# Bias rows of twelve groups instead of eleven ahead of attention, shifted code, and the products of the smallest experts regrouped

## The chip, the cores and the metric

One core of a Trainium2 chip runs the whole program in one launch. The engines that matter here are TensorE (PE in the rows, its weight loads PEld), VectorE (DVE), ScalarE (ACT), GpSimd (POOL) and SyncE (SP), which issues most of the DMAs. The metric is the device time of one execution in microseconds; lower is better.

## The reference

Three layers, one after the other, all in float32:

```python
# 1. attention, B=2, H=8, S=576, D=64, with a learned bias of the relative position
scores = (q @ k.T) / sqrt(D)
x = log1p(|i - j|) / log1p(max(i, 1))              # per row i and column j
bias = relu(x * w1 + b1) @ w2                      # 32 hidden values -> 8 heads
attn = exp(s - max(s)); attn /= attn.sum() + 1e-9  # s = scores + bias
x = attn @ v                                       # -> 1152 tokens x 512

# 2. gated dense layer, 512 -> 1536 -> 512
x = (silu(x @ w_gate) * (x @ w_val)) @ w_out

# 3. top-1 routing over 8 experts, capacity 288 rows, 512 -> 1024 -> 512
e = argmax(x @ gate); out[row] = softmax(x @ gate)[e] * relu(x @ w1[e]) @ w2[e]
```

## The kernel before, in words

**Bias rows.** The bias depends on i only through a factor of the row, so the kernel works on 36 groups of 16 rows. `span(R)` (L103) gives the columns of group R: 400 for R=11, 384 for R=12, 368 for R=13, 352 for R=14. A group takes four VectorE instructions (`bias_t4`, L116, "B" in the tables below), a TensorE product (`bias_mm`, L134, "M", and "MR" for columns past 512), two ScalarE instructions that write the 128x591 tile `bo` (`bias_evac`, L153 and L160, "BE" and "BR"), and a DMA of that tile to the DRAM buffer `bias_d` (L164). Tiles `bo` rotate over four buffers (L145), so a group's L153 writes into the buffer of the group four earlier in the order and needs that group's DMA to have read it. `load_bias` (L168) brings 128 query rows of two heads from `bias_d` back as `bias_sb`, in three DMAs (L175 to L177). Groups are taken in the order R = 16 to 23, 8 to 15, 24 to 31, 0 to 7, 32 to 35; the first eight complete the first 128 query rows.

**Attention.** A lead loop (L377) does the first LEAD = 11 groups (R = 16 to 23 and 8 to 10), interleaved with the first score product, then `keep_warm` (L352, 12 small products with an unused result) and the four B of the next group. A loop of 36 units (L417) follows. Unit u is one pair of heads for 128 query rows: score product "Q" (`qk`, L196, for unit u+1), score plus bias with a row minimum on VectorE ("S0", "S1", L213), exponential on ScalarE ("E0", "E1", L221), row sum and reciprocal ("A" L227, "R" L230), normalising on GpSimd ("N0", "N1", L234), transposes on TensorE ("Ta", "T", "Tb", L263 and L274, of unit u-1) with copies out ("V0", "V1", "Va", "Vb", L280, L285, L287), and the product with v ("AV", L299, of unit u-2, 20 rows of the trace each). Unit u also makes the product and the evacuation of the bias group LEAD+u and the four B of group LEAD+u+1, as long as there are groups; after that come units without any, whose VectorE and ScalarE slots hold the first steps of the next layer's weight decoding (`job`, "JD", "JA", from unit JOB0 on). All instructions stand in the order in which tables of names list them (`FIRST[0]` and `FIRST[1]` for units 0 and 1, `ORDER` for the rest, `LATE0` and `LATE` for units without bias work); each engine runs its own instructions in that order.

**Code position.** `addr_align` (L357) and a table `ALIGN` (L530, used by `align(n)`, L1081) pad the instruction stream of an engine at a few places: a modulus, an offset from the start of a block, and limits.

**Experts.** Experts are sorted by their number of rows. On the inputs here two large ones come first, then one of middle size, one with q=2, and two with q=4, the smallest; the last two are empty. For q=4 `few1` (L1128) does the first product `ps_sh` (L1139), the transposes of the next expert's rows (`transpose_x`, `ps_x`, L1072) and `slots` (L1009), which has a product `ps_c` (L1013), its copy to `sx` on ScalarE (L1014) and a chain on GpSimd that computes the output rows (L1019 to L1024); then VectorE applies relu to `ps_sh` (`hst`, L1150), TensorE transposes it (`ps_st`, L1154) and VectorE copies it to `sht` (L1158). `few2` (L1167) does the second product `ps_sy` (L1179), and `finish` scales it on VectorE (`ob`, L1034) and scatters it to the output (L671).

Of the kernel before, what the change touches and what calls it, by code (L numbers as in the profile page):

```python
# [26 lines left out]
    "R:1 V0:2 S0 AV:3 S1 B E0 V1:2 N0 MR Vb:2 B N1 BR XH:3 E1 B M Ta XL:3 Va Q B T Tb A BE"  # L27
).split()
FIRST = [
    "B B B S0 S1 B E0 MR M BR E1 Q A BE".split(),  # L30
    "R:1 S0 S1 B E0 N0 MR B N1 BR E1 B M Q B Ta Va T Tb A BE".split(),
]
LATE0 = "R:1 V0:2 S0 S1 AV:3 V1:2 JD JD E0 N1 N0 Vb:2 E1 A R XH:3 JA Q XL:3 T".split()
LATE = (
# [5 lines left out]
    "N0 N1 V0:2 V1:2 AV:3 K0 K0 XH:3 XL:3 T T9:2 V2:2 ACT V0 V1 K0 K0 K0 K1 G0 K1 AV T9 XH V2 XL K1 K1 K1 K0 K0 K1 K1 G1".split(),  # L40
    "AV XH XL".split(),
]
LEAD = 11
IDLE = (38, 12)
RAW0 = 18
ZERO0 = 8
JOB0 = 25
GEO0 = 400


def attention(tc, ident, shape, qd, kd, vd, wb, geo, xh, xl, late):
    nc = tc.nc
    B, H, S, D = shape
    P = 128
# [14 lines left out]
    with ExitStack() as ctx:  # L69
# [284 lines left out]
        spare, raw0 = [], []  # L354
        ran = {("Q", 0)}
        with tc.manual_schedule():
            nc.tensor.addr_align(256, offset=164, max_nops=0)  # L357
            keep_warm(IDLE[0], I16)
            first = wk.tile([P, S], F32, tag="bt", name="first", bufs=12)
            nc.scalar.activation(first[:, :1], ident[:, :1], AF.Identity)  # L360
# [15 lines left out]

            for n in range(LEAD):  # L377
                R = groups[n]
# [38 lines left out]
            for u in range(NU + 2):  # L417
# [18 lines left out]
                R, ahead = (groups[n] if n < NG else None for n in (LEAD + u, LEAD + u + 1))  # L436
# [71 lines left out]
def moe_kernel(ctx, tc, shape, qd, kd, vd, wb, geo, wg, wv, wo, g2, e1, e2, ebase, desc, tri, out, cap):  # L508
    nc = tc.nc
    P = 128  # L510
    B, H, S, D = shape
# [15 lines left out]
    BATCHES = (2, 4, 6, 7)  # L527
    FIX, QUADS = 2, 4
    EARLY = 5
    ALIGN = {"tensor": (256, 7, 131, 0, 0), "vector": (128, 45, 100, 0, 0), "scalar": (128, 65, 100, 0, 0)}  # L530
    TINY = float(np.array([0x38100000], np.uint32).view(np.float32)[0])

    cst = ctx.enter_context(tc.tile_pool(name="cst", bufs=1))
# [506 lines left out]
    xd0 = {}  # L1040
# [28 lines left out]
    def transpose_x(e):  # L1069
        if e < NE:  # L1070
            for kc in range(KC):
                nc.tensor.transpose(px[e][:, kc * P:(kc + 1) * P], xd0[e][:, kc * P:(kc + 1) * P], ident)  # L1072
            nc.scalar.copy(xt[e].rearrange("p k t -> p (k t)"), px[e])
# [54 lines left out]
    def few1(e, q):  # L1128
        w = weights(e)
        x = xt[e]  # L1130
        n, fw = P // q, F2 // q
        nk = fw // P
        ph = []
        for s in range(fw // 256):
            ps = eps.tile([P, 512], F32, tag="h", name="ps_sh")
            for kc in range(KC):
                for g in range(q):
                    f = g * fw + s * 256
                    i = nc.tensor.matmul(  # L1139
                        ps[g * n:(g + 1) * n, :256], x[:, kc, :n], w[f // 256][:, kc, :],  # L1140
                        start=kc == 0, stop=kc == KC - 1, skip_group_check=True,
                    )
                    own(i, e, f // 256)
            ph.append(ps)
        to = next_rows(e, q) if q == 4 else None
        h = hst[:, 0]
        pt = []
        for s in range(fw // 256):
            c = slice(s * 256, (s + 1) * 256)
            nc.vector.tensor_scalar_max(h[:, c], ph[s][:, :256], 0.0)  # L1150
            ps = eps.tile([P, 512], F32, tag="t", name="ps_st")
            for k in range(2):
                o = (2 * s + k) * P
                nc.tensor.transpose(ps[:, k * P:(k + 1) * P], h[:, o:o + P], ident)  # L1154
            pt.append(ps)
        ht_ = hid[e][2]
        for s in range(fw // 256):
            nc.vector.tensor_copy(  # L1158
                ht_[:, 2 * s:2 * s + 2].rearrange("p k g t -> p (k g t)"), pt[s][:, :2 * P]
            )  # L1160
        return to

    def next_rows(e, q):
        transpose_x(e + 1)
        return slots(xd0[e], e, 0, q)

    def few2(e, q, to):  # L1167
        w = weights(e)
        n, fw = P // q, F2 // q
        nk = fw // P  # L1170
        to = to or next_rows(e, q)
        ht_ = hid[e][2].rearrange("p k g t -> p (k g t)")[:, :nk * P].rearrange("p (k g t) -> p k g t", k=nk, g=q)
        ps = eps.tile([P, 512], F32, tag="y", name="ps_sy", bufs=3)
        seq = [(k, g) for k in range(nk) for g in range(q)]
        dw = DM // q
        for i, (k, g) in enumerate(seq):
            f = g * nk + k
            for d in range(q):
                m = nc.tensor.matmul(  # L1179
                    ps[d * n:(d + 1) * n, :dw], ht_[:, k, g, :], w[4 + f // 2][:, f % 2, d * dw:(d + 1) * dw],  # L1180
                    start=i == 0, stop=i == len(seq) - 1, skip_group_check=True,
                )
                own(m, e, 4 + f // 2)
        finish(ps, to, dw)
# [122 lines left out]
    with tc.manual_schedule():  # L1307
# [51 lines left out]
        with ExitStack() as nest:  # L1359
            for e in range(FIX, NE):  # L1360
                nest.enter_context(tc.If(ns[e] > (M1 // 2 if e >= QUADS else 0), label=f"q{e}"))
                with tc.If(ns[e] <= M1, label=f"d{e}"):
                    if e < NE - 1:
                        hint(f"q{e + 1}")
                    few2(e, 2, few1(e, 2))
                    load_next(e, False)
            align(4)
        with ExitStack() as nest:  # L1368
            for e in range(QUADS, NE):
                nest.enter_context(tc.If(ns[e] > 0, label=f"z{e}"))  # L1370
                with tc.If(ns[e] <= M1 // 2, label=f"s{e}"):  # L1371
                    few2(e, 4, few1(e, 4))
                    load_next(e, False)


# [80 lines left out]
```

## Time and profile before

| | |
|---|---|
| three runs | 517.97, 519.69, 520.3 us, median 519.69 |
| the profiled execution | 517.11 us, its span 515.5 us, granted clock 0.999 |
| PE busy | 496.0 us (96%) |
| DVE busy | 371.4 us (72%) |
| ACT busy | 266.5 us (52%) |
| POOL busy | 102.3 us (20%) |

The span is the time from the first to the last recorded instruction of the profiled execution; the device time is 1.6 us more. Times of rows below count from the start of the span. Attention ends at about 165 us, the dense layer follows, and the experts take the last part.

### The profile page before, as it was taken

What the parts mean: (1) busy time and instruction counts of PE and PEld (TensorE: products, weight loads), DVE (VectorE), ACT (ScalarE), POOL (GpSimd) and SP (SyncE); (2) the same over time, 40 slices, a digit from 0 to 9 for tenths busy, and PEclk for the clock granted to TensorE, in tenths of its full rate; (3) what the DMA queues carried; (4) which work ended last, traced back from release to release, by engine and by line L of the source; (5) the groups of instructions that cost most, each with busy time, mean ns of one, the idle gap of its engine ahead of it and who ended that gap; (6) DMA issues with size and microseconds to landing.
All of it is one profiled execution on the core that took longest, in us unless ns stands there. A gap on an engine that the chain in (4) does not pass through costs nothing. (4 is left out here: it accounts for less than half of the span.)

```text
span 515.5 us, 12030 instructions
## 1 busy us (share of the span) xinstructions
PE 496.0 (96%) x4414; PEld 413.4 (80%) x4414; DVE 371.4 (72%) x931; ACT 266.5 (52%) x607; POOL 102.3 (20%) x218
## 2 busy tenths in 40 slices
PE   7989999999999999999999999999999899999885
PEld 3467777677868999979999889999777788897654
DVE  6789999997997999996799827644346654644521
ACT  5599899998876445454543203522322344635410
POOL 1054444444552100000000000000013230512112
PEclk9999999999999999999999999999999999999999
DMA  7797779989612944353231000000015799954740
GB/s 267 264 347 276 242 252 330 318 291 343 151 47 59 314 160 133 122 186 100 83 123 41 2 0 1 1 1 0 1 43 167 287 361 405 382 192 130 279 182 10
DMA packets 49937, 88.82 MB, mean 172 GB/s; under 512 B 7954, under 2 KB 27412, under 8 KB 49856
## 3 DMA queue, kind: packets, MB, share of 16 engines
q1 hardware_dynamic: 48416, 84.78, 48.6%
q0 software_dynamic: 1296, 3.03, 1.5%
q8 instruction: 40, 0.66, 0.5%
q14 instruction: 41, 0.34, 0.2%
q10 hardware_dynamic: 144, 0.02, 0.0%
HBM read 66.73 MB, written 22.15 MB: 172 GB/s over the span
## 5 line engine op out<-in xcount | busy, mean ns | idle before, releaser
L587 PE MATMUL ps_gv<-xh,hl 128*128 128x384 f32 x528 | 134.9, 336 | 0.0
L587 PEld LDWEIGHTS ps_gv<-xh,hl 128*128 128x128 f32 x528 | 95.4, 188 | 0.1
L587 PE MATMUL ps_gv<-xl,hl 128*128 128x384 f32 x264 | 88.7, 336 | 0.0
L880 PE MATMUL ps_o<-hl,hh 128*128 128x512 f32 x216 | 72.9, 404 | 0.0
L116 DVE TENSOR_SCALAR bt<-geo_sb 128x320 f32<-128x320 f32 (+17 forms) x144 | 58.4, 454 | 0.0
L221 ACT ACTIVATE e_sb<-e_sb,mn 128x576 f32<-128x576 f32 x72 | 56.4, 784 | 3.9 <-DVE mn L213 3.6
L234 POOL TENSOR_SCALAR e_sb<-e_sb,rs 128x576 f32<-128x576 f32 x72 | 53.3, 751 | 17.5 <-DVE rs L230 14.3
L213 DVE CUSTOM_DVE_ANT_0 e_sb<-ps_s,bias_sb 128x576 f32<-128x576 f32 x72 | 51.6, 751 | 4.3 <-DMA bias_sb<-bias_d 2.3
L671 POOL DMA_INDIRECT disp<-y,rsi x9 | 9.0, 999 | 223.9 <-DVE rs L828 207.8
L587 PEld LDWEIGHTS ps_gv<-xl,hl 128*128 128x128 f32 x264 | 49.6, 188 | 0.1
L880 PEld LDWEIGHTS ps_o<-hl,hh 128*128 128x128 f32 x216 | 40.6, 188 | 10.1 <-issue 1.4
L299 PE MATMUL ps_x<-et,vn 128*64 128x128 f32 (+1 forms) x800 | 47.5, 267 | 0.7 <-DVE xl L317 0.7
L196 PE MATMUL ps_s<-kst,qst 64*128 64x288 f32 (+1 forms) x320 | 46.2, 423 | 0.5 <-DVE mn L213 0.5
L597 ACT CAST hh<-sg 128x384 fp32r<-128x384 f32 x36 | 18.4, 512 | 47.8 <-DVE sg L596 47.7
L299 PEld LDWEIGHTS ps_x<-et,vn 128*64 128x64 f32 x800 | 39.3, 137 | 3.8 <-DVE xl L317 1.0
L880 PE MATMUL ps_o<-hl,hlo 128*128 128x512 f32 x105 | 42.0, 400 | 0.0
L570 ACT CAST hl<-dg 128x512 fp32r<-128x512 f32 x32 | 19.1, 620 | 39.9 <-PE ps_o L880 21.6
L196 PEld LDWEIGHTS ps_s<-kst,qst 64*128 64x128 f32 (+1 forms) x320 | 27.5, 178 | 6.3 <-DVE mn L213 2.2
L263 PEld LDWEIGHTS ps_t<-ident,e_sb 64*128 64x128 f32 x576 | 25.5, 139 | 4.8 <-issue 0.9
L596 DVE TENSOR_TENSOR sg<-ps_gv,sg 128x384 f32<-128x384 f32 x35 | 19.3, 552 | 12.6 <-PE ps_gv L587 12.6
L595 DVE TENSOR_TENSOR sg<-ps_gv,sg 128x384 f32<-128x384 f32 x35 | 19.3, 552 | 10.7 <-ACT sg L594 10.4
L565 ACT ACTIVATE dg<-raw 128x512 f32<-128x512 f32 x32 | 21.0, 673 | 10.0 <-DVE hl L571 7.0
(231 smaller groups left out, 931.4 us busy)
## 6 DMA issues: line engine op xcount, KB each, us to landing
eraw<-e SPq DMA_DIRECT2D x24, 512.0 KB
bias_d<-bo SPq DMA_DIRECT2D x36, 295.5 KB
raw<-e SPq DMA_DIRECT2D x16, 512.0 KB
raw<-wo SPq DMA_DIRECT2D x12, 512.0 KB
raw<-wg SPq DMA_DIRECT2D x11, 512.0 KB
raw<-wv SPq DMA_DIRECT2D x11, 512.0 KB
disp<-zero SPq DMA_DIRECT2D x9, 520.0 KB
bias_sb<-bias_d SPq DMA_DIRECT2D x16, 288.0 KB
```

The source lines that it names most:

```text
L116: nc.vector.tensor_scalar(t[:, :m], dist_sb[:, :m], nbp[:, r:r + 1], None, ALU.max)
L196: nc.tensor.matmul(pss[j][i, half, :HS], qst[c * B + bb][d, p, i], kst[d, bb * NP + p, half * HS:(half + 1) * HS], start=True, stop=True, ...
L213: nc.vector.tensor_tensor_reduce(out=e[:, j, :].rearrange("p (a n) -> p a n", a=2), in0=ps[:, :, :HS], in1=bias_sb[c, p][:, j, :].rearrang ...
L221: nc.scalar.activation(e[:, j, :], e[:, j, :], AF.Exp, bias=mn[:, j:j + 1], scale=-1.0, accum_out=sm[:, j:j + 1])
L234: nc.gpsimd.tensor_scalar(e[:, j, :], e[:, j, :], rs, 1.0, ALU.mult, ALU.mult)
L263: nc.tensor.transpose(tp_t[u, h][:, n * HP:(n + 1) * HP], e[r, n * P:(n + 1) * P], ident[r, r])
L299: nc.tensor.matmul(ps[j * D:(j + 1) * D, o:o + n], vn[:, p, bb, jc, j * D:(j + 1) * D], et[:, t0:t0 + n], start=jc == NF, stop=jc == NF - ...
L565: lambda: nc.scalar.activation(g, hi32.bitcast(F32), AF.Square),
L587: nc.tensor.matmul(ps[:, :TN], w_[:, n, kc, :], x_[:, kc, t * TN:(t + 1) * TN], start=i == 0, stop=i == 3 * KC - 1,)
L595: nc.vector.tensor_tensor(sg, pss[0][:, :TN], sg, ALU.mult)
L596: nc.vector.tensor_tensor(sg, pss[1][:, :TN], sg, ALU.mult)
L880: nc.tensor.matmul(ps, ht_cols(f, a, tg), wot[f][b_], start=i == 0, stop=i == len(ops) - 1)
```

## The change

Five things are changed. LEAD becomes 12, so group R=11 moves from unit 0 into the lead loop, each later group moves to the unit before, and unit 24 becomes one without bias work; JOB0 goes from 25 to 24 with it. The tables of units 0 and 1 are written in another order: unit 0 has its four B later (S0 first), and BE after E1; unit 1 begins with S0 and only then R of unit 0. `keep_warm` after the lead loop has 4 products instead of 12. The code offset of TensorE before attention goes from 164 to 100, and VectorE's offset at `align(2)` from 100 to 109. In the two q=4 experts the copy of 128x256 to `sht` becomes two of 128x128, and `slots` moves from behind the transposes `ps_x` to behind the transposes `ps_st`; for the q=2 expert the order is as before.

```diff
 FIRST = [
-    "B B B S0 S1 B E0 MR M BR E1 Q A BE".split(),
-    "R:1 S0 S1 B E0 N0 MR B N1 BR E1 B M Q B Ta Va T Tb A BE".split(),
+    "MR M S0 S1 E0 B BR B E1 BE Q B B A".split(),
+    "S0 R:1 S1 B E0 N0 MR B N1 BR E1 B M Q B Ta Va T Tb A BE".split(),
 ]
-LEAD = 11
-IDLE = (38, 12)
+LEAD = 12
+IDLE = (38, 4)
-JOB0 = 25
+JOB0 = 24
...
-            nc.tensor.addr_align(256, offset=164, max_nops=0)
+            nc.tensor.addr_align(256, offset=100, max_nops=0)
...
-    ALIGN = {"tensor": (256, 7, 131, 0, 0), "vector": (128, 45, 100, 0, 0), "scalar": (128, 65, 100, 0, 0)}
+    ALIGN = {"tensor": (256, 7, 131, 0, 0), "vector": (128, 45, 109, 0, 0), "scalar": (128, 65, 100, 0, 0)}
...
-        to = next_rows(e, q) if q == 4 else None
+        if q == 4:
+            transpose_x(e + 1)
         h = hst[:, 0]
...
-            nc.vector.tensor_copy(
-                ht_[:, 2 * s:2 * s + 2].rearrange("p k g t -> p (k g t)"), pt[s][:, :2 * P]
-            )
-        return to
-
-    def next_rows(e, q):
-        transpose_x(e + 1)
-        return slots(xd0[e], e, 0, q)
-
-    def few2(e, q, to):
+            if q == 2:
+                nc.vector.tensor_copy(
+                    ht_[:, 2 * s:2 * s + 2].rearrange("p k g t -> p (k g t)"), pt[s][:, :2 * P]
+                )
+            else:
+                for k in range(2):
+                    nc.vector.tensor_copy(
+                        ht_[:, 2 * s + k].rearrange("p g t -> p (g t)"), pt[s][:, k * P:(k + 1) * P]
+                    )
+
+    def few2(e, q):
...
-        to = to or next_rows(e, q)
+        if q == 2:
+            transpose_x(e + 1)
+        to = slots(xd0[e], e, 0, q)
```

TensorE's order at the head, in the lead loop and unit 0 (`ps_w` is the product of a group of the lead loop, `ps_b` that of a group in the unit loop, `ps_s` a score product; - before, + now):

```order
 L196 MATMUL ps_s<-kst,qst 128x288 x4
 L134 MATMUL ps_w_371<-bt,wb_sb 32x416 x4
-L352 MATMUL ps_idle<-ident 128x128 x12
-L134 MATMUL ps_b<-bt,wb_sb 32x400 x4
-L196 MATMUL ps_s<-kst,qst 128x288 x4
+L134 MATMUL ps_w_388<-bt,wb_sb 32x400 x4
+L352 MATMUL ps_idle<-ident 128x128 x4
 L134 MATMUL ps_b<-bt,wb_sb 32x384 x4
 L196 MATMUL ps_s<-kst,qst 128x288 x4
```

The product of the group with 400 columns now stands in the lead loop, ahead of the small products, and unit 0 has that of 384 columns.

ScalarE's order at the same place (`bo` is the bias tile, the rows on `e_sb` are the exponentials of units 0 and 1):

```order
 L160 ACTIVATE bo<-ps_w_371,ncst,geo_sb 128x175
-L221 ACTIVATE e_sb,sm<-e_sb,mn 128x576 x2
-L153 ACTIVATE bo<-ps_b,ncst,geo_sb 128x400
-L160 ACTIVATE bo<-ps_b,ncst,geo_sb 128x191
-L221 ACTIVATE e_sb,sm<-e_sb,mn 128x576 x2
-L280 COPY et<-ps_x 128x64
+L153 ACTIVATE bo<-ps_w_388,ncst,geo_sb 128x400
+L160 ACTIVATE bo<-ps_w_388,ncst,geo_sb 128x191
+L221 ACTIVATE e_sb,sm<-e_sb,mn 128x576 x2
 L153 ACTIVATE bo<-ps_b,ncst,geo_sb 128x384
```

The evacuation of the group with 400 columns moved ahead of the two exponentials of unit 0, and behind these now stands that of the group with 384 columns.

TensorE's order in the first of the q=4 experts, with what each row waits for; before:

```order
L1072 MATMUL ps_x<-ident,xd_5476 128x128 x3
L1013 MATMUL ps_c<-xd_5475,copies_3131 128x2 [waits DMAHW3_49,Activation_49]
L1154 MATMUL ps_st<-ident,hst 128x128 [waits DVE_49]
L1154 MATMUL ps_st<-ident,hst 128x128
L1179 MATMUL ps_sy<-eraw_5515,sht 32x128 [waits DMAHW2_49,DVE_49]
```

and now:

```order
L1072 MATMUL ps_x<-ident,xd_5466 128x128 x3
L1155 MATMUL ps_st<-ident,hst 128x128 [waits DVE_49]
L1155 MATMUL ps_st<-ident,hst 128x128
L1013 MATMUL ps_c<-xd_5465,copies_3121 128x2 [waits DMAHW3_49,Activation_49]
L1183 MATMUL ps_sy<-eraw_5505,sht 32x128 [waits DMAHW2_49,DVE_49]
L1183 MATMUL ps_sy<-eraw_5505,sht 32x128 x3
```

The product `ps_c` went from ahead of the two transposes of `hst` to behind them.

## Rows read from the trace of the kernel before

**Rows 1.** Busy time by stretch: stretch, length, engines' busy us (instructions), PEclk, DMA share, GB/s.

```profile
20.00:30.00 10.00, 8.80 (x81) 5.70 (x73) 6.22 (x20) 5.64 (x14) 2.11 (x4) 1.00 0.96 297
320.00:360.00 40.00, 40.00 (x233) 40.00 (x232) 19.46 (x35) 12.75 (x25) 0.00 (x0) 1.00 0.00 1
...
514.00:515.50 1.50, 0.00 (x0) 0.00 (x0) 0.00 (x0) 0.00 (x0) 0.00 (x0) 0.80 0.00 0
```

**Rows 2.** Timeline of TensorE: start, length, line, operation, xcount [idle before <- releaser].

```profile
34.32 1.31 PE L299 MATMUL ps_x<-et,vn 128*64 128x128 f32 x20
...
57.28 1.31 PE L299 MATMUL ps_x<-et,vn 128*64 128x128 f32 x20
...
131.24 1.31 PE L299 MATMUL ps_x<-et,vn 128*64 128x128 f32 x20
...
147.41 1.31 PE L299 MATMUL ps_x<-et,vn 128*64 128x128 f32 x20
```

**Rows 3.** Timeline of VectorE, S0 of units 0 and 24.

```profile
23.38 0.76 DVE L213 CUSTOM_DVE_ANT_0 e_sb<-ps_s,bias_sb 128x576 f32<-128x576 f32 x1 [1.99 <-DMA bias_sb<-bias_d]
...
117.30 0.76 DVE L213 CUSTOM_DVE_ANT_0 e_sb<-ps_s,bias_sb 128x576 f32<-128x576 f32 x1 [0.30 <-DMA bias_sb<-bias_d]
```

**Rows 4.** Timeline of SyncE, issues of the bias DMAs near 22 and 106 us.

```profile
19.01 0.32 SPq L175 DMA_DIRECT2D bias_sb<-bias_d  x1
...
22.59 1.40 SPq L164 DMA_DIRECT2D bias_d<-bo  x3
...
28.32 0.91 SPq L176 DMA_DIRECT2D bias_sb<-bias_d  x1
...
106.65 0.77 SPq L164 DMA_DIRECT2D bias_d<-bo  x1
114.34 0.33 SPq L175 DMA_DIRECT2D bias_sb<-bias_d  x1
```

**Rows 5.** Timeline of ScalarE, evacuation of the bias group of unit 0.

```profile
26.38 0.67 ACT L153 ACTIVATE bo<-ps_b,ncst,geo_sb 128x400 f32<-128x400 f32 x1
26.95 0.50 ACT L160 ACTIVATE bo<-ps_b,ncst,geo_sb 128x191 f32<-128x191 f32 x1
```

**Rows 6.** Timeline of TensorE, bias products of units 1 and 2.

```profile
27.50 0.85 PE L134 MATMUL ps_b<-bt,wb_sb 128*32 128x384 f32 x8 [0.64 <-ACT bo L160]
...
31.04 0.82 PE L134 MATMUL ps_b<-bt,wb_sb 128*32 128x368 f32 x8 [0.72 <-ACT bo L160]
```

**Rows 7.** Busy time by stretch again, columns as in the first group.

```profile
23.40:26.60 3.20, 2.64 (x17) 1.13 (x16) 1.84 (x5) 1.86 (x5) 0.00 (x0) 1.00 1.02 363
```

**Rows 8.** DMA issues: line, count, KB each.

```profile
bias_d<-bo SPq DMA_DIRECT2D x36, 295.5 KB
...
bias_sb<-bias_d SPq DMA_DIRECT2D x16, 288.0 KB
```

**Rows 9.** DMA queues from 19.5 to 20.5 us: packets, MB, share of 16 engines' time.

```profile
q8 instruction: 1, 0.02, 6.0%
```

**Rows 10.** Timeline of TensorE in the two q=4 experts.

```profile
500.96 0.38 PE L1013 MATMUL ps_c<-xd,copies 32*128 32x2 f32 x2
501.27 0.44 PE L1154 MATMUL ps_st<-ident,hst 128*128 128x128 f32 x2
502.23 1.95 PE L1179 MATMUL ps_sy<-eraw,sht 128*32 128x128 f32 x64 [0.52 <-DVE sht L1158]
...
507.33 0.44 PE L1154 MATMUL ps_st<-ident,hst 128*128 128x128 f32 x2
```

**Rows 11.** Timeline of VectorE in the second of these experts.

```profile
506.85 0.42 DVE L1150 TENSOR_SCALAR hst<-ps_sh 128x256 f32<-128x256 f32 x1 [2.19 <-PE ps_sh L1139]
...
510.37 0.35 DVE L1034 TENSOR_SCALAR ob<-ps_sy,sx 128x128 f32<-128x128 f32 x1 [2.14 <-PE ps_sy L1179]
```

**Rows 12.** Groups by line and shape, VectorE: count | busy us, mean ns | idle before.

```profile
L285 DVE COPY et<-ps_t 128x512 f32<-128x512 f32 x36 | 24.4, 677 | 0.4 <-PE ps_t L263 0.4
L1158 DVE COPY sht<-ps_st 128x256 f32<-128x256 f32 x4 | 1.7, 424 | 1.5 <-PE ps_st L1154 1.5
```

More of the change, by code (lines that the diff above doesn't have):

```diff
@@ L1364, in moe_kernel @@
                         hint(f"q{e + 1}")
-                    few2(e, 2, few1(e, 2))
+                    few1(e, 2)
+                    few2(e, 2)
                     load_next(e, False)
@@ L1371, in moe_kernel @@
                 with tc.If(ns[e] <= M1 // 2, label=f"s{e}"):
-                    few2(e, 4, few1(e, 4))
+                    few1(e, 4)
+                    few2(e, 4)
                     load_next(e, False)
```

## The prediction

> **What bounds the kernel now.** I read the busy time by stretch first. In a stretch of the dense layer TensorE is busy for all of its 40 us at a granted clock of 1.00; at the head, from 20 to 30 us, it has 8.80 of 10 while the DMA share is 0.96 [rows 1]. So TensorE sets the time except at the two ends: at the head it is held by DMAs, and at the tail by short chains through VectorE and ScalarE. The clock falls only in the last 1.5 us, with no TensorE work left [rows 1]. That narrows the change to four places: the head, the bias units of attention, one late DMA wait, and the two smallest experts.
>
> Next comes TensorE's timeline of the product with v, which occurs once a unit and so gives the period. From 34.32 to 57.28 six units take 22.96 us, 3.83 each, and these hold a bias product; from 131.24 to 147.41 five units without one take 16.17 us, 3.23 each [rows 2]. VectorE's timeline then shows two waits for bias tiles: 1.99 us before the first S0 and 0.30 us before that of unit 24 [rows 3]. SyncE's timeline tells which DMA is meant, and the last views read are the experts' timelines.
>
> **The change part by part.** The sum is made against the profiled execution's 517.11 us and then carried to the median 519.69, which is 2.58 us higher; the rows explain no part of that gap.
>
> *One bias unit fewer.* The product, the evacuation and the four B of one group leave the unit loop. The groups that follow move one unit up, so one unit of 3.83 us becomes one of 3.23: -0.60 [rows 2]. The work that left stands in the lead loop: the product takes the place of idle products on TensorE, and ScalarE and VectorE wait there, VectorE for 1.99 us [rows 3]. It costs nothing as long as the first S0 still waits for its DMA. If a unit is held by VectorE and not by TensorE, the gain may come out at nothing.
>
> *The wait at unit 24.* Its bias tile was loaded at 114.34, when the write of the last group it needs, issued at 106.65, had landed [rows 4]. That write is now issued one unit, about 3.8 us, earlier. The 0.30 us go [rows 3]: -0.30, at worst 0, if another engine is late at the same point.
>
> *The first evacuation in unit 0.* Here the change adds a wait. Before, unit 0 evacuated the 400-column group from 26.38 on [rows 5], into a `bo` buffer read out long before. Now it evacuates the 384-column group, whose buffer is that of the fourth group before it, and that group's DMA is the first of the three issued from 22.59 on [rows 4], behind two loads of 128 query rows. When does it land? S0 of unit 0 starts at 23.38 [rows 3] with half of the first load there; left are the other half of 288 KB, the second load of 576 KB and the write of 295.5 KB [rows 8], 1160 KB. From 23.40 to 26.60 the DMAs moved 363 GB/s [rows 7], so 3.2 us carry 1160 KB, and the write lands at 26.6 if the queues run evenly: +0.2 against 26.38. From the other side: the L176 load at 28.32 [rows 4] waits, in SyncE's order, for the same write, so by 28.3 it was there: at most +1.9. Behind the evacuation ScalarE holds the exponentials of unit 1, and TensorE's next bias product waits for it, by 0.64 us at 27.50 and again by 0.72 at 31.04 for the one after [rows 6]; score product, transposes and the next evacuation follow in that chain, so its delay reaches the end undiminished. I take 27.0, +0.6, nearer to the even landing than to the bound, since the DMA share stays at about 1 [rows 7].
>
> The Trainium skill ("DMA: Bandwidth & Descriptors", section "Why a DMA increments its semaphore by 16 and not by 1") says that a copy is spread over up to 16 engines which finish independently, and that only the full count means that all data has landed. By that rule the slowest engine decides and the even estimate of 26.6 is too early; with the rule the term is +0.6 or more, without it +0.2. The trace of before shows only the bounds.
>
> *Rest of the head.* S0 of unit 0 no longer has three B before it in its unit, but all four of its group stand in the lead loop: one more ahead of a wait of 1.99 us [rows 3], so 0. R after S0 in unit 1: 0, since S0 of unit 0 is what unit 0's exponentials wait for and R of that unit is not due before. Four idle products instead of twelve: 0, they ran in TensorE's idle time.
>
> *Code offsets.* From 19.5 to 20.5 us the trace has one instruction fetch, and it took 6.0% of 16 engines [rows 9], 0.96 us of one DMA engine. It falls into the first bias load, issued at 19.01 [rows 4]. With the offset of 100 the boundary moves to a later instruction, out of this load: if the load's slowest engine was the one with the fetch, S0 of unit 0 starts up to 0.8 us sooner; if the fetch then lies on the write that the evacuation waits for, up to 0.96 later. No row tells which. I take 0, with -0.8 and +1.0 as ends. VectorE's offset moves by nine instructions: 0, within the same ends.
>
> The Trainium skill ("Runtime: NRT & Kernel Launch", section "Instruction fetch mechanics") has an engine fetch blocks of 256 instructions with a DMA queue of its own while it executes. By it the offset is worth nothing; the row shows a fetch that takes a whole microsecond of one DMA engine while the others carry data, by which it is worth up to 0.96.
>
> *The two smallest experts.* In the first, `ps_c` runs from 500.96 and holds up the transposes, which start at 501.27: without it they start 0.31 earlier; `ps_c` then runs in the time in which TensorE waits for the copy, 0.52 us [rows 10]. In the second the transposes, at 507.33, wait for `hst`, which ends at 507.27 [rows 10, 11], so nothing there. The copy: 128x512 takes 677 ns and 128x256 424 [rows 12], 0.99 ns a column; a half of 128 columns takes 424 - 127 = 297 ns. The second half lies beside the first half of the products, 32 of 64 rows or 0.97 us [rows 10]. So -0.13 in each expert, and -0.31 - 0.26 = -0.57 in all. On GpSimd the chain for the output rows starts about half a microsecond later; it has until the result is scaled, at 510.37 in the second expert [rows 11], 2 us after the products begin. Bounds: a half copy at half the price, -0.31 - 0.42 = -0.73; a half that costs as much as the whole, -0.31.
>
> Sum: -0.60 - 0.30 + 0.60 + 0 - 0.57 = -0.87, so 516.24 for the profiled execution, and 519.69 - 0.87 = **518.8 us** on the median.
>
> **The rivals.**
>
> *The evacuation holds unit 0 (slower).* Place: L153 of unit 0. If the write lands only at 28.3, the term is +1.9 instead of +0.6, and the sum +0.43: 520.1 us. It decides from a start of 27.9 on (26.38 and the 1.47 that the other terms save). For it: the DMA share of about 1 [rows 7] and the load that waits until 28.32 [rows 4]. Against it: that SyncE row is an upper bound, since it may have waited for its place in the issue order alone.
>
> *The fetch leaves the first load (faster).* S0 of unit 0 starts 0.8 sooner, and the write lands with the queues at 26.6 or before, so the term of the evacuation is +0.2 or less: -0.60 - 0.30 + 0.2 - 0.57 - 0.8 = -2.07, 517.6 us. For it: the 6.0% [rows 9] inside a load that VectorE waits for. Against it: nothing shows that this engine was the last.
>
> *The clock falls in the head.* TensorE has eight products fewer in its idle time. If it were granted the lower level, 1.2 instead of 2.4 GHz, for the bias products of units 1 and 2, these would take 0.85 + 0.82 us more [rows 6]: -0.87 + 1.67 = +0.80, 520.5 us. For it: 0.80 granted in the idle last 1.5 us; against it: 1.00 from 20 to 30 us, in spite of 1.2 us idle [rows 1].
>
> The Trainium skill ("TensorE: Matmul & The Clock Gate", section "HAM oscillation — how this bites in real kernels") says that waits for data between products can bring the clock down. The trace agrees only at its end; at the head none is seen.
>
> *The unit gains nothing.* If VectorE bounds the units that now move, only the other terms stay: -0.27, 519.4 us.
>
> **How the numbers follow.** Chances: the forecast 0.50, with a range of its own from 518.0 to 519.6; the evacuation 0.14; the fetch 0.20; the clock 0.04; no gain from the unit 0.12. A difference under 0.5% (2.6 us) can't be told from no change with this kernel. To be faster by more, under 517.1, the fetch's gain must meet the other terms at their ends, or the true level of before be below its median: 0.16. To be slower by more, over 522.3, takes the fetch on the late write and the clock together: 0.05. The range reaches from 516.8, the fetch with the tail's best end and the write early, to 520.9, the evacuation with part of a fetch on its write.
>
> **What the profile after would show.** Right: 23 units with 3.8 and a first unit of 3.2 one earlier, S0 of unit 24 without a wait; L153 of unit 0 at about 27.0 with a DMA of `bias_d` as its releaser; in both experts the wait before `ps_sy` at some 0.4 and `ps_c` inside it. Wrong: L153 after 27.9, a fetch that moves S0 of unit 0 off 23.4, a granted clock under 1.00 before 40 us, or a new wait on GpSimd before the scatter.

## The result: slower, at the head by the clock as much as by the wait

The changed kernel has a median of 521.78 us over 14 runs (519.51 to 524.86), the kernel before 518.02 over 14; the ratio is 1.0066, 95% interval 1.0043 to 1.0089. Measured again (run 9 below) it is 1.0053 [1.0027, 1.0079]. Forecast were 518.8 us and a range up to 520.9: the time lies outside and on the other side. The forecast stood on the median of three runs, 519.69; over 14 runs the kernel before is 1.67 us below that, so the medians differ by +3.76 us where -0.87 was forecast.

The profiled execution of the changed kernel took 519.51 us, its span 517.9, 2.4 us over the profiled one before. So it is one of the two quickest of the 14; what the others have on top comes up with run 9. Three places of it answer to the prediction. ScalarE at the head (start, length, line, operation, in brackets the idle time before it and what ended that):

```profile
24.14 0.78 ACT L221 ACTIVATE e_sb<-e_sb,mn 128x576 f32<-128x576 f32 x1
...
27.81 0.67 ACT L153 ACTIVATE bo<-ps_b,ncst,geo_sb 128x384 f32<-128x384 f32 x1 [2.80 <-DMA bias_d<-bo]
```

Unit 0's evacuation stands idle for 2.80 us, and the DMA that ends this is the write of the tile of group R=8, from the buffer that it reuses. (R=8 is the ninth group in the order; the expectations below count from zero and call it the eighth.) Before, its counterpart began at 26.38 with no wait [rows 5]. TensorE at the same place:

```profile
23.34 2.06 PE L196 MATMUL ps_s<-kst,qst 64*128 64x288 f32 x8
28.95 1.20 PE L134 MATMUL ps_b<-bt,wb_sb 128*32 128x368 f32 x8 [3.56 <-ACT bo L160]
30.08 2.29 PE L196 MATMUL ps_s<-kst,qst 64*128 64x288 f32 x8
...
37.05 1.31 PE L299 MATMUL ps_x<-et,vn 128*64 128x128 f32 x20
```

It has nothing to do for 3.56 us, where it had 0.64 [rows 6]; then the product of 368 columns takes 1.20 us instead of 0.82, and the score product behind it 2.29, where a later one (at 35.32) takes 1.24. The windows tell why (stretch, length, busy us of PE, PEld, DVE, ACT and POOL with instruction counts, granted clock, DMA share, GB/s):

```profile
26.00:27.00 1.00, 0.00 (x0) 0.00 (x0) 1.00 (x6) 0.00 (x0) 0.76 (x2) 1.00 1.04 399
27.00:28.00 1.00, 0.00 (x0) 0.00 (x0) 1.00 (x3) 0.19 (x1) 0.79 (x1) 1.00 1.20 369
28.00:29.00 1.00, 0.05 (x4) 0.05 (x8) 0.61 (x2) 1.00 (x3) 0.00 (x0) 1.00 0.92 333
29.00:30.00 1.00, 1.00 (x8) 0.10 (x8) 0.00 (x0) 1.00 (x3) 0.00 (x0) 0.63 1.08 359
30.00:31.00 1.00, 1.00 (x8) 0.79 (x6) 0.17 (x1) 0.41 (x2) 0.22 (x1) 0.50 0.91 344
31.00:32.00 1.00, 1.00 (x6) 0.63 (x6) 0.00 (x0) 0.00 (x0) 0.99 (x2) 0.50 1.06 395
32.00:33.00 1.00, 1.00 (x20) 0.81 (x16) 0.60 (x1) 0.49 (x2) 0.48 (x1) 0.66 1.01 356
```

TensorE idles through 26 to 28, and just as it starts again the granted clock falls to 0.50, which is 1.2 GHz, for some three microseconds. From 20 to 30 us the kernel before had 1.00 [rows 1]. The first product with v starts at 37.05 instead of 34.32 [rows 2]: +2.73 us at the head. Of these 1.43 are the later start of the evacuation (27.81 against 26.38), and 1.30 come between it and that product (9.24 us against 7.94).

From there the units win part of it back. The dense layer's first product after attention, before and now:

```profile
166.72 0.44 PE L587 MATMUL ps_gv<-xh,th 128*128 128x384 f32 x1
168.66 0.44 PE L587 MATMUL ps_gv<-xh,th 128*128 128x384 f32 x1
```

That is +1.94, so the unit loop gave 0.79. The small drift up to the middle expert is +0.22. Then comes a place of which the prediction said nothing would happen, TensorE's wait at the branch into the q=2 expert (TensorE's waits near the end: line, releaser, total, times, longest):

```profile
PE ps_sh L1139 <- DVEq L1366: 2.4, 1, 2.4
PE ps_mh L1203 <- DVEq L1349: 1.2, 1, 1.2
PE ps_sh L1139 <- DVEq L1363: 1.1, 1, 1.1
```

The first of these was 1.64 us in the kernel before (timeline of TensorE there):

```profile
488.05 3.67 PE L1139 MATMUL ps_sh<-raw,xt 128*64 128x256 f32 x32 [1.64 <-ACTq L1362]
```

Now VectorE's sequencer is the last to come, and the wait is 2.37 us: +0.73. The two smallest experts do what was forecast:

```profile
503.91 0.44 PE L1155 MATMUL ps_st<-ident,hst 128*128 128x128 f32 x2
504.28 0.38 PE L1013 MATMUL ps_c<-xd,copies 32*128 32x2 f32 x2
504.73 1.95 PE L1183 MATMUL ps_sy<-eraw,sht 128*32 128x128 f32 x64
...
510.23 0.38 PE L1013 MATMUL ps_c<-xd,copies 32*128 32x2 f32 x2
510.68 1.95 PE L1183 MATMUL ps_sy<-eraw,sht 128*32 128x128 f32 x64
```

`ps_c` lies inside the wait for the copy, and `ps_sy` shows no idle time where it had 0.52 [rows 10]; the shift against before goes from +2.89 at the first of these experts to +2.39 at the last product. Sum: 2.73 - 0.79 + 0.22 + 0.73 - 0.50 = 2.39, the difference of the spans (2.4).

### The profile page after: what moved, and what is told of

Read it like the earlier page. It is cut to its first block, busy times and chain, and to the rows that moved or that the text cites. A ratio compares the mean times of both kernels' runs of the same rounds, so it can differ in the third digit from the quotient of the medians.

```text
span 517.9 us, 11999 instructions
## 1 busy us (share of the span) xinstructions
PE 494.6 (96%) x4397; PEld 411.4 (79%) x4397; DVE 371.1 (72%) x933; ACT 266.5 (51%) x606; POOL 102.3 (20%) x218
## 5 line engine op out<-in xcount | busy, mean ns | idle before, releaser
L196 PEld LDWEIGHTS ps_s<-kst,qst 64*128 64x128 f32 (+1 forms) x320 | 27.4, 182 | 6.6 <-DVE mn L213 1.3
L134 PE MATMUL ps_b<-bt,wb_sb 128*32 128x512 f32 (+11 forms) x192 | 23.9, 569 | 4.3 <-ACT bo L160 4.2
## 6 DMA issues: line engine op xcount, KB each, us to landing
bias_d<-bo SPq DMA_DIRECT2D x36, 295.5 KB, 4.1
```

Of the source, the lines that this page charges most:

```text
L134: nc.tensor.matmul(ps[t4 * GW:(t4 + 1) * GW, :m1 - m0], wb2, bt_t[R, t4][:, m0:m1], start=True, stop=True)
L196: nc.tensor.matmul(pss[j][i, half, :HS], qst[c * B + bb][d, p, i], kst[d, bb * NP + p, half * HS:(half + 1) * HS], start=True, stop=True, ...
```

## The experiments

Theory A: the head loses by the wait for the write of R=8, and once more because TensorE idles behind it and its clock falls. Rival B: the clock falls for want of the eight idle products. Rival C: the code offsets carry the loss. Ratios are those to the kernel before on the same chip, with 95% intervals. They need not equal the quotient of two medians (up to 0.3% apart). Runs 1 to 4, 5 to 8, 9 to 12 and 13 to 16 shared a chip each. Five kernels were measured twice: four repeat their ratio within 0.13%, but that of runs 12 and 14 differs by 0.54%. So a single difference of half a per cent between two chips shows little; pairs on one chip count for more.

**Run 1, the evacuation into a buffer nobody has used.**

```diff
-                bo_t[R] = wk.tile([P, WIDE], F32, tag="bo", name="bo", bufs=4)
+                bo_t[R] = (
+                    wk.tile([P, NB_ * P], F32, tag="et", name="bo", bufs=3)[:, :WIDE] if R == groups[LEAD]
+                    else wk.tile([P, WIDE], F32, tag="bo", name="bo", bufs=4)
+                )
```

> The changed kernel, but the 384-column group of unit 0 is evacuated into a buffer of another tag (et) that nobody has used yet, so its first activation waits for no DMA. Theory A (the loss is that wait, and TensorE's clock falls because TensorE idles behind it): the evacuation starts right after the second exponential of unit 0, at 25.0 instead of 27.8; TensorE's longest idle before 32 us falls from 3.56 to about 1.5 us; granted clock 1.00 until 40 us; the first product with v starts near 34 instead of 37.05; about 517 us, some 1 below the kernel before and 4 to 5 below the changed one. Rival B (the clock falls for the eight idle products that are gone): clock still at 0.5 to 0.7 near 30 us, 520 us or more. Rival C (the loss is in the code offsets): as the changed kernel, 521.8 us.

Measured: 518.50 us, 0.9993 [0.9970, 1.0015], 1.5 us over what theory A forecast. The head is as theory A has it: no wait, evacuation at 25.49, first product with v at 33.28 instead of 37.05, granted clock 1.00 from 26 to 50 us.

```profile
26.61 0.83 PE L134 MATMUL ps_b<-bt,wb_sb 128*32 128x368 f32 x8 [0.64 <-ACT bo L163]
```

TensorE's wait is back at the 0.64 us of [rows 6]. Of the 3.78 us by which the dense layer starts sooner than in the changed kernel (164.88 against 168.66) 2.7 are left at the end (spans 515.2 and 517.9), since the branch before the q=2 expert now costs more than in the changed kernel (its line numbers are 3 higher here):

```profile
PE ps_sh L1142 <- DVEq L1369: 3.4, 1, 3.4
```

**Run 2, idle products in the wait.**

```diff
+                if u == 0:
+                    for _ in range(11):
+                        nc.tensor.matmul(beside()[:, 3 * P:], ident, ident, start=True, stop=True)
```

> The changed kernel plus 11 idle products of 128x128 on TensorE behind the score product of unit 1, in the time in which it waits for that evacuation; the wait itself stays. Theory A: evacuation still at 27.8, granted clock 1.00 until 40 us, bias product of unit 1 at about 28.9 as in the changed kernel, but the first product with v at some 35.7 instead of 37.05; 519 us, so the clock is worth 1.3 us in a run like the profiled one and 2 to 3 us in the median. Rival C: no difference, 521.8. If the idle products delay the real ones the first product with v is not earlier than 37.

Measured: 519.81 us, 1.0019 [0.9996, 1.0042]. The wait stays (evacuation at 27.39, 1.92 us for the DMA), the clock does not fall there, and the first product with v starts at 35.19:

```profile
25.79 2.72 PE L502 MATMUL ps_x<-ident 128*128 128x128 f32 x22
28.52 0.83 PE L134 MATMUL ps_b<-bt,wb_sb 128*32 128x368 f32 x8
29.28 1.24 PE L196 MATMUL ps_s<-kst,qst 64*128 64x288 f32 x8
```

```profile
28.00:32.00 4.00, 3.27 (x43) 2.10 (x45) 2.69 (x9) 3.35 (x10) 1.90 (x4) 1.00 1.00 351
```

So in this profile the clock held where TensorE had work during the wait, and the evacuation still waited for its DMA. This execution's clock fell in another place, behind a 3.5 us wait for VectorE at the q=2 expert:

```profile
490.00:494.00 4.00, 3.73 (x20) 2.71 (x22) 0.04 (x1) 0.00 (x0) 0.00 (x0) 0.57 1.00 381
```

**Run 3, VectorE's offset back.**

```diff
-    ALIGN = {"tensor": (256, 7, 131, 0, 0), "vector": (128, 45, 109, 0, 0), "scalar": (128, 65, 100, 0, 0)}
+    ALIGN = {"tensor": (256, 7, 131, 0, 0), "vector": (128, 45, 100, 0, 0), "scalar": (128, 65, 100, 0, 0)}
```

> The changed kernel with VectorE's code offset back at 100 instead of 109. Theory A with its second part (the offset alone lengthens the branch before the q=2 expert): TensorE's wait before the first product of that expert falls from 2.37 to 1.64 us, the rest of the trace as in the changed kernel, 521.1 us. Rival: the wait comes from the code that moved in the experts or from TensorE's side, and stays at 2.4 us; 521.8 us.

Measured: 519.41 us, 1.0011 [0.9987, 1.0036], 1.7 us under the forecast. The wait at the q=2 expert is 1.6 us as expected; the evacuation still waits, until 27.45, with the clock at 0.50 from 30 to 32 us.

**Run 4, the small experts alone.** The kernel before with the diff in `few1` and `few2`, nothing else.

> The kernel before with only the change in the two q=4 experts (halves of the copy, the small product behind the transposes). Theory A: head as before, clock 1.00; the wait before the second product falls from 0.52 to about 0.15 us in both experts, the transposes of the first start 0.3 us sooner; from the start of the first of these experts to the end 0.5 us less; 517.5 us, which a comparison of medians can hardly tell from 518.0. Rival: the chain on GpSimd, half a microsecond later, holds the scatter, and nothing is gained: 518.0 or more.

Measured: 518.25 us, 0.9992 [0.9965, 1.0019]: too little to be seen in the times. In the profile the lag behind before shrinks from 1.57 us at the q=2 expert to 1.03 at the last `ps_sy`: 0.54 us, near the 0.57 of the sum.

**Run 5, the kernel before with VectorE's offset 109.** One number: `"vector": (128, 45, 109, 0, 0)`.

> The kernel before with nothing but VectorE's code offset 109 in place of 100. Theory A': the offset alone makes VectorE late at the branch ahead of the q=2 expert, so TensorE's wait there is 2.4 to 3.5 us instead of 1.64, in some executions with a clock of 0.5 for some 3 us behind it; 0.8 to 2.5 us slower than the kernel before, near 520. Head and attention as before, clock 1.00 until 40 us. Rival (the late branch comes from the changed order of the experts' code or varies by chance): wait 1.6 to 1.8, 518.8 us, no difference.

Measured: 519.78 us, 1.0002 [0.9977, 1.0026], a miss in time. The profile shows the wait at 2.2 us and a fall behind it, so the mechanism exists, but it doesn't move the median:

```profile
PE ps_sh L1139 <- DVEq L1362: 2.2, 1, 2.2
```

```profile
488.00:492.00 4.00, 4.00 (x24) 2.87 (x22) 0.42 (x1) 0.00 (x0) 0.18 (x1) 0.57 1.00 366
```

**Run 6, own buffer and offset 100 together** (the edits of runs 1 and 3).

> The changed kernel with both suspects taken out: own buffer for the first evacuation of unit 0, VectorE's offset 100. Theory A': evacuation at 25 to 25.5, clock 1.00 in the head, first product with v near 33.3, wait before the q=2 expert 1.64 us; 518.5 of the run with the buffer alone less 1.8 (3.44 - 1.64): 516.7, some 2 us (0.4%) below the kernel before. Rival (the two losses are not independent, or attention's gain is given back in the dense layer): 518 or more.

Measured: 516.81 us, 0.9944 [0.9914, 0.9975], as forecast; evacuation at 24.72, first product with v at 32.52, wait at the q=2 expert 1.6.

**Run 7, the write ahead of the second bias load**, with offset 100.

```diff
                     load_bias(order[0], 0)
-                    load_bias(order[0], 1)
+                elif n == GPC:
+                    load_bias(order[0], 1)
                 elif n == GPC + 1:
```

> The changed kernel with VectorE's offset 100, and the second load of 128 bias rows issued behind the write of the eighth group instead of ahead of it; buffers as in the changed kernel. Theory A' (the write was late because 576 KB stood before it in the queue): evacuation of unit 0 right after the second exponential, at about 25 to 25.5 with no DMA as its releaser, clock 1.00 in the head, first product with v at 33.3 to 34; 516.7 to 517.5. Rival (the write is late for another reason, such as one slow DMA engine): evacuation still after 27, clock below 1, 519.4 as with the offset alone. If the second load is now late, S0 of unit 2 waits for it.

Measured: 515.79 us (6 runs), 0.9928 [0.9901, 0.9955]. The evacuation starts at 25.92 with nothing to wait for (the write was issued at 21.21 and landed 3.6 us later), the clock is 1.00 in the head. The queue's order alone had made the write late. But this profile has a fall in a third place, at the first products of the experts (`ps_h`, from 414.27 on), and so has run 14's; TensorE had stood idle there for 0.46 and 0.55 us at most since 408 us:

```profile
415.00:418.00 3.00, 3.00 (x14) 3.00 (x14) 0.83 (x3) 0.92 (x2) 0.00 (x0) 0.50 0.97 320
```

**Run 8, TensorE's offset back** to 164.

> The changed kernel with TensorE's code offset back at 164. If the offset is what brought S0 of unit 0 from 23.4 to 22.5 (the fetch left the first bias load), it goes back to 23.2 or later; the evacuation waits for its DMA as before, until 27.5 to 28.5, TensorE idles a little less than 3.56 us, clock falls; 521.8 within 1 us either way. Rival (the gain at S0 comes from the order of the tables): S0 at 22.5 to 22.9 still.

Measured: 519.70 us, 1.0004 [0.9987, 1.0021], a miss: 2.1 us under the forecast, and level with the kernel before. S0 of unit 0 is at 23.48, as expected if the fetch counts, but by a TensorE product and not a DMA; and the kernel before, with 164, had it at 23.38 in one profile and 22.52 in another (run 5). The fetch itself did move with the offset, as the prediction had it: in all six profiles with 164 one lies at 19 to 21 us on the queue of [rows 9], in none of the twelve with 100 (in the changed kernel it lies at 31). But S0 starts at 22.5 to 23.5 in the six and at 22.2 to 23.4 in the twelve. So what the offset does to S0 is not shown. The evacuation waits until 26.94, TensorE idles 1.71 us, and the clock falls all the same, to 0.50 from 28 to 34 us.

**Run 9, the changed kernel again.**

> The changed kernel once more, beside the next three on one chip. Theory A': 0.4 to 0.8% above the kernel before; mean granted clock of its executions about 0.990 against 0.997; in the profile a fall to 0.5 behind the wait for the eighth group's write (evacuation of unit 0 at 27 to 28), and in executions with a clock of 0.990 a second one. Rival (the first measurement drew a bad chip): ratio within 0.3% of 1.

Measured: 521.31 us, 1.0053 [1.0027, 1.0079], mean granted clock of its executions 0.991 against 0.997. The profiled execution, 521.52, lies at the median and has two falls:

```profile
28.00:32.00 4.00, 3.80 (x24) 1.95 (x26) 0.55 (x3) 1.66 (x5) 1.69 (x3) 0.50 1.00 337
32.00:34.00 2.00, 1.57 (x24) 0.85 (x21) 2.00 (x6) 1.99 (x5) 0.00 (x0) 0.50 1.02 386
491.00:495.00 4.00, 3.69 (x20) 2.67 (x22) 0.42 (x1) 0.00 (x0) 0.14 (x1) 0.61 1.01 382
```

The second follows a wait of 2.8 us for VectorE at the q=2 expert: that expert's first product ends 1.69 us later than its start would have it. In this execution that makes up most of the 2 us over the first profile. The other executions have no profile. Eight of the twelve have a mean clock of 0.990 or less, which is some 10 us or more at the lower level and longer than any one fall seen here, so most fell more than once; where is not known.

**Run 10, twelve idle products again** (`IDLE = (38, 12)`).

> The changed kernel with 12 idle products after the lead loop again instead of 4. Theory A': the idle time that counts is the one behind the evacuation, from 25.4 to 29 us, and these products end before it; wait, fall of the clock and time as in the changed kernel, within 0.3%. Rival B: the eight products were what kept the clock up; clock 1.00 until 40 us, 1.5 to 3 us faster than the changed kernel.

Measured: 519.27 us, 1.0036 [1.0005, 1.0068]. This is a miss for theory A as I had put it, and a point for rival B. The wait stays (evacuation at 27.43), but 12 products last until 25.1, push the real ones back, and TensorE idles 1.44 us instead of 3.56:

```profile
22.10 2.94 PE L352 MATMUL ps_idle<-ident 128*128 128x128 f32 x24
25.10 0.85 PE L134 MATMUL ps_b<-bt,wb_sb 128*32 128x384 f32 x8
25.89 1.24 PE L196 MATMUL ps_s<-kst,qst 64*128 64x288 f32 x8
28.56 0.82 PE L134 MATMUL ps_b<-bt,wb_sb 128*32 128x368 f32 x8 [1.44 <-ACT bo L160]
```

The clock holds, and the first product with v is at 35.20. That is where run 2 has it (35.19) with four idle products, so in this profile the eight products cost nothing at the head and covered the wait. Five of the 12 executions are at 522.65 or more, with clocks of 0.995 and less; so the cover does not hold every time. Against run 9 on the same chip the median is 2.0 us lower, but the two intervals overlap.

**Run 11, the head alone:** the kernel before with LEAD 12, the two tables, the idle products and JOB0.

> The kernel before with only the twelve groups: tables of units 0 and 1, LEAD, the idle products and JOB0; code offsets and experts as before. Theory A': all of the head's loss is there: evacuation of unit 0 with a DMA as its releaser at 27 to 28, clock at 0.5 for some 4 us behind it, first product with v 2 to 2.7 us later than in the kernel before, of which the unit loop gives back 0.8; without the offsets' and with none of the tail's part 0.2 to 0.5% slower than before. Rival C (offsets): same as before within 0.2%.

Measured: 519.01 us, 1.0013 [0.9985, 1.0041], mean clock 0.9935. In the profiled execution, one of the quickest (517.26), the wait was short, 0.52 us, and the clock held; the slower ones are at 0.989 to 0.992. By its ratio this is within what rival C forecast and below theory A's 0.2%, and on the same chip the whole change (run 9) takes 2.3 us more; the intervals overlap.

**Run 12, the write ahead with offset 109**, run 7's edit alone on the changed kernel.

> The changed kernel with nothing but the second load of bias rows behind the eighth group's write; VectorE's offset stays at 109. Theory A': head without a DMA wait and with a clock of 1.00, as with the offset of 100; 4 to 5 us faster than the changed kernel beside it and 0.3 to 0.6% below the kernel before. If VectorE's offset costs what single profiles show (0.7 to 1.9 us and at times the clock), it stays 1 to 2 us behind the 0.9928 that the same with an offset of 100 measured; if not, it reaches that ratio.

Measured: 518.55 us, 0.9999 [0.9973, 1.0026]; head as in run 7 (24.77, clock 1.00), the wait at the q=2 expert 1.7. It differs from run 9, on the same chip, by the place of one load alone and is 2.8 us faster; 4 to 5 were forecast, and a time below the kernel before, so this is a miss in size.

**Runs 13 to 16, on one chip:** the write ahead with offset 100, the same with 109, the kernel before with 109, and the changed kernel with 100 (run 3's kernel).

> The version with the write ahead of the second bias load and VectorE's offset 100, a second time, on one chip with the next three. Theory A': 0.5 to 0.7% faster than the kernel before, mean granted clock about 0.997; no fall in the head, wait before the q=2 expert 1.6 us.

> The same with VectorE's offset 109. Theory A' (the offset costs a longer wait before the q=2 expert and in many executions a fall of the clock behind it): 0.4 to 0.7% slower than the one with 100 beside it, mean clock lower by 0.002 to 0.003. Rival (the pairs so far differed by their chips): within 0.2% of it.

> The kernel before with VectorE's offset 109, a second time. Theory A': as with the other pair 0.3 to 0.7% slower than before. Rival (the offset costs only together with the new code of the small experts, as the first run of this kernel, at 1.0002, says): within 0.2% of the kernel before.

> The changed kernel with VectorE's offset 100 and the second bias load ahead of the write, as in the changed kernel: against the first of these four it shows the price of the wait alone. Theory A': 0.6 to 0.8% slower than the first (wait 1.4 to 2.8 us, clock about 0.992 against 0.997), so within 0.2% of the kernel before. Rival (the wait alone is worth less than 1 us, the rest is the offset): at most 0.3% slower than the first.

| run | median us | ratio to before | evacuation | first product with v | mean clock |
|---|---|---|---|---|---|
| 13, no wait, 100 | 515.95 | 0.9934 [0.9910, 0.9958] | 25.15 | 32.94 | 0.996 |
| 14, no wait, 109 | 517.23 | 0.9945 [0.9928, 0.9963] | 25.34 | 33.13 | 0.995 |
| 15, before, 109 | 519.42 | 1.0006 [0.9983, 1.0029] | 25.92 | 33.86 | 0.996 |
| 16, wait, 100 | 519.86 | 1.0010 [0.9984, 1.0036] | 28.41 | 37.80 | 0.992 |

On this chip the kernel before has a mean clock of 0.996 too, and 24 of its 35 executions lie at 0.996 or less: it has falls of its own, which no kept profile of it shows.

Run 16 against run 13 differs by the place of one load in the queue: 519.86 - 515.95 = 3.9 us. The first row is run 13's, where the write was issued at 20.35 and landed 3.7 us later; the others are run 16's:

```profile
25.15 0.65 ACT L153 ACTIVATE bo<-ps_b,ncst,geo_sb 128x384 f32<-128x384 f32 x1
28.41 0.67 ACT L153 ACTIVATE bo<-ps_b,ncst,geo_sb 128x384 f32<-128x384 f32 x1 [3.52 <-DMA bias_d<-bo]
```

```profile
29.55 1.46 PE L134 MATMUL ps_b<-bt,wb_sb 128*32 128x368 f32 x8 [4.27 <-ACT bo L160]
30.93 2.22 PE L196 MATMUL ps_s<-kst,qst 64*128 64x288 f32 x8
```

The wait is longest of all, and again both products behind it run at little more than half speed. That is theory A, priced on one chip each time: 3.9 us with offset 100, and 2.8 with 109 (runs 9 and 12).

VectorE's offset stays open. With 109 the wait at the q=2 expert is 1.7 to 3.5 us in ten profiles, and in four of them (runs 2, 5, 9 and 14) the clock falls behind it; with 100 it is 1.6 to 1.8 in eight profiles, and never does. In times, run 14 against 13, on one chip, gives 1.3 us in the medians and 0.1% in the ratios (inside both intervals), runs 5 and 15 nothing against the kernel before: by the ratios what the rivals had forecast for runs 14 and 15, and not theory A. Between chips, runs 3 and 16 against the changed kernel give some 0.5%, and run 12 against 7 gives 0.7%. Whether it costs anything in the median is not settled.

Nor is rival C as a whole. One at a time, the own buffer (0.9993), idle products in the wait (1.0019), VectorE's offset (1.0011 and 1.0010), TensorE's offset (1.0004) and the queue's order (0.9999 and 0.9945) each bring the changed kernel's 1.0066 and 1.0053 down to about the kernel before or below it. Together that is more than the whole loss, so either the gains don't simply add or part of them is a difference of the chips. Beyond the price of the wait on one chip, how the loss divides stays open.

## Why the prediction was wrong

**The step that failed is the term of the first evacuation in unit 0.** The prediction saw the wait and its place, but took +0.60 for it; the first product with v came +2.73 later, 1.43 by the start of the evacuation and 1.30 by the clock behind it. The rival of the evacuation came nearest, but 27.81 stays under its own mark of 27.9; its term of +1.9 holds for neither part alone. Two things were wrong in the step.

*The start.* I took 27.0, between the even landing at 26.6 and the bound of 28.3 [rows 4, 7]. In the eight profiles with the wait the evacuation starts at 26.5 to 28.4, 27.81 in the first. The bound rested on a SyncE row of which the trace shows no wait for that write. The reason for the even landing, a DMA share of about 1, says nothing of whose bytes move. Between S0 and the evacuation, from 22.46 to 27.81, the profile of the changed kernel has

```profile
DMA packets 951, 1.66 MB, mean 311 GB/s; under 512 B 247, under 2 KB 247, under 8 KB 950
```

where 1.16 MB at 363 GB/s were counted: half a megabyte more went by before the write was done, and at a lower rate. And the comparison with 26.38 hid the price: without the wait (runs 1, 6, 7, 12, 13, 14) it starts at 24.7 to 25.9, so the wait costs about 2.1 us (mean 27.4 against 25.2) of what the change could have had. The page "DMA: Bandwidth & Descriptors" of the Trainium skill says, in the section "Why a DMA increments its semaphore by 16 and not by 1", that only the full count means that all data has landed; it pointed the right way, but no run here shows the single engines.

*The clock.* I gave it a rival of its own at 0.04, argued with the 1.2 us that TensorE idled from 20 to 30 us in the kernel before [rows 1], and never asked how long it would idle behind the wait that I had just added. S0 of unit 0 came 0.92 us sooner (22.46 against 23.38 [rows 3]), with eight idle products fewer, so the score product was done at 25.4 and the wait stood bare: 3.56 us. From the evacuation to the first product with v it takes 7.8 us where the clock holds (runs 1, 2, 10, 11 and 13) and 8.9 to 9.5 where it falls (the changed kernel, runs 3, 8, 9 and 16): 1.1 to 1.7 us, which comes on top of the delay and only together with it. The size of that rival was right (1.67); two rivals that share a cause were priced as if only one could happen.

The page "TensorE: Matmul & The Clock Gate" of the Trainium skill (section "HAM oscillation — how this bites in real kernels") describes just that: a wait for data between products, and the next ones run cold. The runs agree, though length alone does not tell: the clock fell after 1.71 us idle in run 8 and held after 3.44 us at the q=2 expert in run 1.

*The idle products.* Four instead of twelve were taken as 0, since they ran in TensorE's idle time. In run 10, with twelve, the clock held behind the same wait in the profile, and the first product with v came 1.85 us sooner than at 37.05; the wait that the change adds made them worth something.

**Code offsets, taken as 0.** For TensorE the fetch left the first load as the prediction had it, and what that gave is not shown (run 8). For VectorE the trace moved by +0.73 at one branch, within the bound of +1.0, but the bound was taken for the fetch's time alone, and a fall of the clock behind it (1.69 us in run 9) was not in it. The rule of the page "Runtime: NRT & Kernel Launch" of the Trainium skill (section "Instruction fetch mechanics"), by which the offset is worth nothing in straight code, has a second half on branches outside the fetched blocks that would fit here: at a branch VectorE's wait was 1.6 to 1.8 us with one offset and 1.7 to 3.5 with the other. That a fetch is its cause no run shows.

**What was right.** One bias unit fewer and the wait at unit 24: -0.90 forecast, -0.79 in the profile, where S0 of unit 24 waits for no DMA any more but 0.26 us for its score product. The small experts: -0.57 forecast, -0.50 and -0.54 (run 4). S0 of unit 0 as in the rival of the fetch, 0.92 against 0.8; as its cause is not shown, that the size fits may be luck, and the gain went straight into the longer wait. Of the prediction's signs of being wrong two came, S0 off 23.4 and a clock under 1.00. The chance of 0.05 for slower by more than half a per cent looks too low, for the same reason as the clock's. The low end of the range, 516.8, needs the evacuation 0.46 us ahead of 26.38, for which no row stands.

So the profile's +2.39 lies 3.26 from the forecast -0.87: 2.13 by the step that failed, 0.73 by VectorE's wait at the q=2 expert, 0.22 by the drift, and 0.18 by gains that came out a little smaller. The median's +3.76 has more on top, which only run 9's profile shows in part.

With the two causes taken away the change is worth having: run 13 measures 0.9934 [0.9910, 0.9958] and run 7 0.9928, some 3.5 to 4 us below the kernel before. Only a load and a write have changed places in the queue, and one offset is as it was.

## What to carry to other kernels

When work moves one slot ahead, follow its buffers too: the tile that it writes may still be on its way out, in a queue behind larger transfers that nobody hurried. Price a new wait by what the engines could have done without it, and look at what TensorE does meanwhile: if it has just become idle, add the products behind the wait at half clock. Idle products that look useless may be what covers such a wait.

## What the runs showed of the hardware

- A fall of the granted clock to 0.50 lasted 3 to 7 us and cost 1.1 to 1.7 us each time, at the head, and 1.69 at the q=2 expert (run 9); whole executions can be told by it: in run 9 those at 0.993 to 0.996 took 518.5 to 520.5 us, those at 0.990 and less 520.7 to 524.0.
- At the head and the q=2 expert the wait of TensorE at such a fall was between 1.71 us (run 8) and 4.27 us (run 16), while 3.0 and 3.4 us (runs 10 and 1, at the q=2 expert) passed without one; near 415 us it fell in runs 7 and 14 with no wait over 0.55 us since 408 us.
- A load of 576 KB ahead of a write of 295.5 KB in the queue delayed what depended on the write by 3.3 us in one pair of profiles (runs 16 and 13) and by about 2 us in the means of eight profiles with and six without it, at a DMA share of about 1.
